# Block-sparse attention followed by a SwiGLU block: dense masked scores replaced by per-block lists of key blocks

## The chip, the cores and the metric

One Trainium2 chip, and of it one core. The time of a kernel is the device time of one execution in microseconds (us). Lower is better. A profile shows one execution, from its first to its last instruction (the span).

## What is computed

Attention over 4 batches of 8 heads, 768 positions, 64 values per head, then RMS normalisation and a SwiGLU feed-forward block. Positions are grouped in 24 blocks of 32. A query block may attend to its neighbours at a distance of at most one block, to the first and the last block, and to three sampled blocks that arrive as data. The first and the last query block attend to everything.

```python
B, H, S, D = q.shape                      # 4, 8, 768, 64
scores = scale * np.matmul(q, k.transpose(0, 1, 3, 2))
mask = np.abs(blk_i - blk_j) <= 1
mask = mask | (blk_i == 0) | (blk_j == 0) | (blk_i == n_blocks - 1) | (blk_j == n_blocks - 1)
for qb in range(n_blocks):
    for kb in sampled_blocks[qb]:         # three per query block, known at run time alone
        mask[qb * 32:(qb + 1) * 32, kb * 32:(kb + 1) * 32] = True
attn = softmax(np.where(mask, scores, -1e9));  x = attn @ v        # heads side by side: 3072 x 512
xn = x / rms(x) * rms_g
out = (silu(xn @ w_gate) * (xn @ w_val)) @ w_out                   # 512 -> 1536 -> 512
```

## The kernel before

The work is cut into 24 tiles of 128 queries (six a batch) and these into ten units: batch 0 has three units of one tile and one of three, every other batch two of three. A unit goes through attention, normalisation and the feed-forward block.

Scores are dense. The mask is folded into the product: each head's 64 rows of K and of Q are widened by 24 rows (one per block), so that one matmul over 88 rows gives the score plus 0 for an allowed pair of blocks, and a large negative number for the rest. `aug` holds the widened rows as they come from memory (`fill`, `fillk`, `fillq`), `X` the same turned: in batch 0 by TensorE transposes (`tpx` L258, copied out by `evx`), later by a DMA transpose issued on SP (`turn` L245). Positions are dealt to partitions so that one load piece is 1536 contiguous bytes. For a unit of `nt` tiles, `qk` (L276), `exp` (L296) and `av` (L310) do, for each pair of heads and each of the six key tiles:

```python
nc.tensor.matmul(out=s_[:, e, j * w:(j + 1) * w],                  # qk: w = nt * 128 columns
                 lhsT=x[0:KQ, 0, e, jt * P:(jt + 1) * P],
                 rhs=x[0:KQ, 1, e, c0 * P:c0 * P + w], start=True, stop=True)
nc.scalar.activation(out=pts[u, pr][...], in_=s_[...], func=AF.Exp, scale=SCALE)
nc.tensor.matmul(out=o_[:, t, e, :], lhsT=pt[:, jt, e, t * P:(t + 1) * P],   # av: 65 columns
                 rhs=va[:, (2 * pr + e) * NC + jt, 0:D + 1], ...)  # column 65 of V is 1: the row sum
```

V stays in SBUF (`vaug`, filled by `pad_v`). `xo` (L321, L322) divides by the row sum, `sq`, `rsq` (on POOL, L343) and `xq` (L350) normalise, `tr` (L361) and `cp`, or from unit 4 on a DMA transpose `xt` (L376), turn the tile. The feed-forward block is `proj` (L388, gate and value, 12 column groups for a unit of three tiles), `th` (L397, ACT), `uu` (L403, DVE), `hp` (L414, DVE), `yy` (L427) and `yo` (L437, ACT or DVE), with the store on SP. The weights are loaded and cast to 16 bits by DMAs that POOL issues: `load_w` (L211, four quarters of gate and value) and `load_wo` (L215, two halves).

The order of all of it is written down when the program is built. Each piece is an `op` with a cost for each engine that may do it, things it waits for, buffers and PSUM banks that it takes and frees, and a priority. A planner loop deals them out by their earliest start; what it deals is recorded at once, so each engine's queue is a fixed order, and an engine waits wherever the chip is later than the plan. `idle` (L128) puts matmuls without use into the TensorE queue where the plan expects TensorE to wait early on. `gate_sync` holds the loads of batch 1 on the SP queue until parts of the weights have landed.

Of the kernel before, what the change touches and what calls it, by code (L numbers as in the profile page):

```python
# [17 lines left out]
def kernel(  # L18
# [11 lines left out]
):  # L30
    nc = tc.nc
    SIMOUT = None
# [3 lines left out]
    NC = S // P  # L36
    DM = H * D
# [3 lines left out]
    MASKV = -32768.0  # L41
    SCALE = 1.0 / (D ** 0.5)
    NRND = sampled_blocks.shape[1]
    KQ = D + NB
    NSLOT, NAUG, NRAW, NOPEN = 5, 2, 3, 2
    AHEAD, HURRY, HURU = 0.8, ("av", "xo", "sq", "rsq", "xq", "tr", "cp"), 0
    NSTARV, ZPAT, NG2 = 3, 32.0, 4
    AH = {"uu": 0.3, "hp": 0.3}
    WARM = (11, 10, 2)
    HD = NC * D // 2  # L50
    UNITS = [(0, 0, 1), (0, 1, 1), (0, 2, 1), (0, 3, 3)]
    UNITS += [(b, c, 3) for b in range(1, B) for c in (0, 3)]
    NU = len(UNITS)
    HG = [(b, c // 3) for b, c, n in UNITS]
# [5 lines left out]
    psum = ctx.enter_context(tc.tile_pool(name="psum", bufs=1, space=bass.MemoryType.PSUM))  # L60
    PS = psum.tile([P, 8, 512], FP32, name="PS")

    def bank16(n):
        return PS[:, n].bitcast(BF16)

    qv = q.rearrange("b h (p c) d -> b p h (c d)", c=NC)
    kv = k.rearrange("b h (p c) d -> b p h (c d)", c=NC)
    vv = v.rearrange("b h (p c) d -> b p h (c d)", c=NC)

    raws = {}  # L70
    aug = [const.tile([P, 2, 2, NC, P], BF16, name=f"aug{i}") for i in range(NAUG)]
    XA = const.tile([P, NSLOT, 2, 2, S], BF16, name="XA")
    X = [XA[:, i] for i in range(NSLOT)]
    vaug = [const.tile([P, H * NC, D + 2], BF16, name=f"vaug{i}") for i in range(2)]

    def load(g, i):
        b, pr = divmod(g, NP)
        if i == 0:
            raws[g] = raw.tile([P, 3, 2, NC * D], FP32, name="qkv", tag="qkv")
        nc.sync.dma_start(out=raws[g][:, i], in_=(kv, qv, vv)[i][b, :, 2 * pr:2 * pr + 2, :])  # L80

    TI = work.tile([P, DM], I32, name="ti", tag="yo", bufs=3)
    TF = work.tile([P, DM], FP32, name="tf", tag="yo", bufs=3)
    TB = work.tile([P, 2 * DM], BF16, name="tb", tag="yo", bufs=3)
    samp_i = TI[0:32, 200:200 + 2 * NRND]
# [3 lines left out]
    nc.scalar.dma_start(out=samp_i[0:NB, :], in_=s64)  # L89
    A = [raw.tile([P, 3, 2, NC * D], FP32, name="qkv", tag="qkv") for g in range(3)]  # L90
    def load0(g, i, e=slice(0, 2), x=None, eng=nc.sync):
        x = x or slice(0, HD if i == 1 else NC * D)
        eng.dma_start(
            out=A[g][:, i, e, x], in_=(kv, qv, vv)[i][0, :, 2 * g:2 * g + 2][:, e, x])

    load0(0, 0, slice(0, 1))
    load0(0, 0, slice(1, 2))
    load0(0, 1, x=slice(0, D), eng=nc.scalar)
    load0(0, 1, x=slice(D, HD))
    load0(1, 0)  # L100
    load0(1, 1)
    gB = const.tile([P, DM], FP32, name="gB")
    scr = const.tile([P, 16], BF16, name="scr")
    scf = const.tile([P, 1], FP32, name="scf")
# [9 lines left out]
    zt = const.tile([P, 512], BF16, name="zt")  # L114
    nc.vector.memset(zt[:, 0:P], 0.0)  # L115
    kmask = const.tile([P, NC, NB], BF16, name="kmask")
    nc.vector.memset(kmask, 1.0)
    ident = const.tile([P, P], BF16, name="ident")
    nc.vector.memset(ident, 0.0)
    Bm = TB[0:32, 0:32]  # L120
    nc.vector.memset(Bm, 1.0)
# [4 lines left out]
    def idle(n, bk=7):  # L126
        for i in range(n):
            nc.tensor.matmul(out=PS[:, bk, 0:P], lhsT=zt[:, 0:P], rhs=zt[:, 0:P], start=True, stop=True)  # L128

    idle(WARM[0])  # L130
    ji = TI[0:32, 0:NRND * 32].rearrange("p (r j) -> p r j", r=NRND)
    nc.gpsimd.iota(ji, pattern=[[0, NRND], [1, 32]], base=0, channel_multiplier=0)
    nc.gpsimd.affine_select(
        out=kmask, in_=kmask, compare_op=ALU.is_ge, fill=0.0,
        base=0, pattern=[[1, NC], [-32, NB]], channel_multiplier=NC)
# [664 lines left out]
```

## Time and profile before

| what | value |
|---|---|
| three runs | 309.01, 309.51 and 314.6 us; median 309.51 us |
| the profiled execution, first to last instruction | 307.2 us (its own total is not listed; the median of the runs lies 2.3 us above its span) |
| busy: TensorE matmul (PE), weight load (PEld) | 299.6 us (98%), 200.2 us |
| busy: ACT, DVE, POOL | 203.7, 192.3, 24.4 us |
| scores, L276 | 480 matmuls, 81.1 us busy |
| exponentials, L296 | 192 instructions (188 in pt, 4 in ph), 145.8 us |
| probabilities times V, L310 | 1152 matmuls |
| gate and value, L388; output, L427 | 960 and 300 matmuls |
| DMA | 42.42 MB in 70,661 packets |

PE is TensorE's matmul row, PEld its weight load, DVE VectorE, ACT ScalarE, POOL GpSimd, SP the queue that issues most DMAs; L276 is line 276 of the kernel. A matmul's duration is its latency and overlaps the next one's, so what one costs is read from runs of equal matmuls in the chain of waits (36 of L310 in 1.15 us), not from its mean.

### The profile page before, as it was taken

To read this page: it belongs to the slowest core of one execution; us is meant where nothing else is said; L and a number is where in the kernel's file an instruction comes from. 1 tells how busy PE (TensorE), PEld (TensorE's weight loads), DVE (VectorE), ACT (ScalarE), POOL (GpSimd) and SP (SyncE) were. 2 spreads that over 40 slices of the span, in tenths; PEclk is the share of its full clock that TensorE was granted. 3 is DMA by queue.
4 is the path that set the end of the run, shared out by engine and by line. 5 is a ranking of instruction groups with operands and counts; after the bars stand their busy time and mean duration, and the time that the engine had idled before them with its cause. 6 is when DMAs were issued, how large, how long until landed. Compare 5 with 4: busy or idle time off the path is not lost.

```text
span 307.2 us, 7350 instructions
## 1 busy us (share of the span) xinstructions
PE 299.6 (98%) x3033; PEld 200.2 (65%) x3062; DVE 192.3 (63%) x435; ACT 203.7 (66%) x319; POOL 24.4 (8%) x43
## 2 busy tenths in 40 slices
PE   8999999999999999999999999999999999999994
PEld 7998888766666566666666666666666546556543
DVE  6687766857779678756754753674389607727500
ACT  5999875678977878787877787878833143233221
POOL 3566000100001001001000100010000000000000
PEclk9999999999999999999999999999999999999999
DMA  7999999999999999940894030003010050010022
GB/s 207 370 231 172 215 268 228 228 333 247 262 285 271 227 205 222 242 155 3 173 157 101 0 87 2 34 3 85 2 36 1 20 158 12 0 70 0 0 105 104
DMA packets 70661, 42.42 MB, mean 138 GB/s; under 512 B 48356, under 2 KB 67556, under 8 KB 70628
## 3 DMA queue, kind: packets, MB, share of 16 engines
q1 hardware_dynamic: 64528, 37.17, 49.2%
q0 software_dynamic: 5792, 4.72, 10.0%
q8 instruction: 24, 0.39, 0.6%
q10 hardware_dynamic: 308, 0.07, 0.1%
q14 instruction: 9, 0.07, 0.1%
HBM read 28.57 MB, written 6.29 MB: 114 GB/s over the span
## 4 chain that ended last, share of the span: by engine, by line
PE 96%; ACT 2%; issue 1%; DVE 0%; ACTq 0%
PE PS L388 40%; PE PS L276 20%; PE PS L427 20%; PE PS L310 12%; PE PS L258 2%; ACT pt L296 1%; PE PS L128 1%; PE PS L361 0%; ACT th L397 0%; PE PS L153 0%; ACT yo L437 0%; PE PS L183 0%; DVE zt L115 0%; ACTq L437 0%
## 5 line engine op out<-in xcount | busy, mean ns | idle before, releaser
L296 ACT ACTIVATE pt<-PS 128x768 bf16<-128x768 f32 x188 | 142.8, 812 | 32.2 <-PE PS L276 31.5
L403 DVE SCALAR_TENSOR_TENSOR uu<-th,PS 128x384 bf16<-128x384 bf16 x96 | 53.0, 554 | 58.7 <-ACT th L397 55.7
L276 PE MATMUL PS<-XA 88*128 88x384 bf16 (+1 forms) x480 | 81.1, 293 | 0.7 <-ACT pt L296 0.6
L388 PE MATMUL PS<-xn,wv 128*128 128x384 bf16 (+1 forms) x480 | 75.5, 293 | 0.0
L388 PE MATMUL PS<-xn,wg 128*128 128x384 bf16 (+1 forms) x480 | 75.1, 294 | 0.0
L397 ACT ACTIVATE th<-PS 128x384 bf16<-128x384 f32 x96 | 47.2, 493 | 34.8 <-PE PS L388 32.1
L427 PE MATMUL PS<-wo,hp 128*128 128x512 bf16 (+1 forms) x271 | 65.4, 370 | 1.5
L414 DVE TENSOR_TENSOR hp<-uu,PS 128x384 bf16<-128x384 bf16 x96 | 51.4, 551 | 14.2 <-PE PS L388 14.0
L388 PEld LDWEIGHTS <-wv 128*128 128x128 bf16 x480 | 41.6, 97 | 23.3
L388 PEld LDWEIGHTS <-wg 128*128 128x128 bf16 x480 | 41.4, 98 | 22.5
L276 PEld LDWEIGHTS <-XA 88*128 88x128 bf16 x480 | 39.2, 97 | 21.4 <-issue 1.8
L427 PEld LDWEIGHTS <-hp 128*128 128x128 bf16 x300 | 29.1, 98 | 27.0
L310 PEld LDWEIGHTS <-pt 128*128 128x128 bf16 x1128 | 40.5, 97 | 5.8
L310 PE MATMUL PS<-vaug,pt 128*128 128x65 bf16 x1128 | 42.1, 193 | 0.0
L437 ACT ACTIVATE yo<-PS 128x512 f32<-128x512 f32 (+1 forms) x22 | 12.7, 578 | 27.9 <-PE PS L427 27.2
L343 POOL TENSOR_TENSOR rs<-ms,nhalf 128x3 f32<-128x3 f32 (+1 forms) x10 | 7.9, 785 | 203.8 <-DVE ms L335 203.8
L322 DVE TENSOR_TENSOR xo<-PS,rz 128x384 f32<-128x384 f32 (+1 forms) x40 | 19.1, 478 | 1.4
L350 DVE SCALAR_TENSOR_TENSOR xq<-xo,rs,gB 128x512 bf16<-128x512 f32 x24 | 17.3, 747 | 2.3 <-POOL rs L343 2.3
L335 DVE CUSTOM_DVE_ANT_0 sc<-xo 128x512 bf16<-128x512 f32 (+1 forms) x24 | 16.1, 669 | 0.2
L321 DVE RECIPROCAL rz<-PS 128x6 f32<-128x6 f32 (+1 forms) x40 | 7.4, 186 | 12.8 <-PE PS L310 12.6
L112 DVE CAST aug<-qkv 128x768 bf16<-128x768 f32 (+1 forms) x28 | 14.5, 538 | 0.1
L112 DVE COPY XA<-PS 88x768 bf16<-88x768 bf16 (+2 forms) x17 | 8.4, 516 | 2.3 <-PE PS L258 2.2
(60 smaller groups left out, 74.5 us busy)
## 6 DMA issues: line engine op xcount, KB each, us to landing
out_dram<-yo SPq DMA_DIRECT2D x23, 256.0 KB, 2.4
qkv<-in_v_dram SPq DMA_DIRECT2D x15, 384.0 KB, 6.1
qkv<-in_k_dram SPq DMA_DIRECT2D x14, 384.0 KB, 5.6
qkv<-in_q_dram SPq DMA_DIRECT2D x12, 384.0 KB, 5.7
wg<-in_moe_w_gate_dram POOLq DMA_DIRECT2D x4, 384.0 KB, 7.3
wv<-in_moe_w_val_dram POOLq DMA_DIRECT2D x4, 384.0 KB, 8.4
wo<-in_moe_w_out_dram POOLq DMA_DIRECT2D x2, 768.0 KB, 19.0
q<-in_q_dram SPq DMA_DIRECT2D x1, 768.0 KB
```

The lines of the kernel that those rows point to most:

```text
L112: nc.vector.tensor_copy(out=out, in_=in_)
L276: nc.tensor.matmul(out=s_[:, e, j * w:(j + 1) * w], lhsT=x[0:KQ, 0, e, jt * P:(jt + 1) * P], rhs=x[0:KQ, 1, e, c0 * P:c0 * P + w], start=T ...
L296: nc.scalar.activation(out=pts[u, pr][:, g * kt:(g + 1) * kt].rearrange("p j e w -> p e j w"), in_=s_[:, :, 0:kt * w].rearrange("p e (j w) ...
L310: nc.tensor.matmul(out=o_[:, t, e, :], lhsT=pt[:, jt, e, t * P:(t + 1) * P], rhs=va[:, (2 * pr + e) * NC + jt, 0:D + 1], start=(jt == 0), ...
L322: nc.vector.tensor_tensor(out=xos[u][:, :, 2 * pr:2 * pr + 2, :], in0=o_[:, :, :, 0:D], in1=rz.unsqueeze(3).to_broadcast([P, nt, 2, D]), o ...
L335: nc.vector.tensor_tensor_reduce(out=sc[:, z], in0=x, in1=x, scale=1.0 / DM, scalar=mss[u][:, 0:1] if nt == 1 and t else 1e-6, op0=ALU.mul ...
L350: nc.vector.scalar_tensor_tensor(out=xqs[u][:, t, :], in0=xos[u][:, t].rearrange("p h d -> p (h d)"), scalar=mss[u][:, t:t + 1], in1=gB, o ...
L388: nc.tensor.matmul(out=p_[:, j, :].rearrange("p (t w) -> p t w", w=P), lhsT=w_[:, c, f_ * P:(f_ + 1) * P], rhs=xns[u][:, :, c, :], start=( ...
L397: nc.scalar.activation(out=t_, in_=tiles["gp", u, f], func=AF.Tanh, scale=0.5)
L403: nc.vector.scalar_tensor_tensor(out=t_, in0=tiles.pop(("th", u, f)), scalar=1.0, in1=tiles.pop(("gp", u, f)), op0=ALU.add, op1=ALU.mult)
L414: nc.vector.tensor_tensor(out=hps[u][:, f * fg:(f + 1) * fg, :], in0=tiles.pop(("uu", u, f)), in1=tiles.pop(("vp", u, f)), op=ALU.mult)
L427: nc.tensor.matmul(out=tiles["yp", u, t, h], lhsT=hps[u][:, f, t * P:(t + 1) * P], rhs=wo[:, f, x], start=(f == 0), stop=(f == NF - 1))
```

## The change

Attention is rewritten; the feed-forward block, its lines (L388 becomes L538, L427 becomes L577) and the units of work stay. The order of tiles inside a batch becomes 5, 0, 1, 2, 3, 4, and tile 5, written `AT`, now holds query blocks 0, 23, 21 and 22; tile n holds blocks 4n+1 to 4n+4.

- A tile's keys. For each of the four query blocks x of a tile, `kg` slot x is a list of 128 keys: three sampled blocks and one fixed block. Two more slots (4 and 5), each shared by two query blocks, hold two neighbour blocks and the first and last block. `kg_fixed` copies the fixed parts (four copies for each half tile, on DVE or ACT). `kg_sampled` copies the sampled ones, one instruction a block, at an address read from a table in a register (half on POOL, half on ACT, each preceded by one register instruction).
- A tile's values. `store_v` writes V with its column of ones as rows of 1040 bytes to DRAM (`vrows`). `gather_v` fetches for one query block the 128 rows of its list by an indirect DMA on POOL, with row numbers `idx` that the start of the kernel computes on DVE; entries that repeat point to rows of zeros. `pair_v` loads the shared slots by plain DMAs on SP.
- Scores. `q_diag` lays the queries of two heads block-diagonally (`qbd`), so that one matmul over 128 rows gives both heads: four matmuls of 64 columns and two of 128 for a pair of heads of an ordinary tile. `AT` has six matmuls of 128 columns over all keys for blocks 0 and 23, and two of 64 and one of 128 for its other blocks (`qka`).
- `exp` then has two instructions of 512 values for four heads (`expa` has four of 512, 256, 64 and 128 values for two heads); `av` has 24 matmuls for four heads of an ordinary tile and 36 for `AT`, each of 65 columns as before.
- K is turned for two heads at a time without padding; K, V and Q are loaded in pieces of 512, 512 and 256 bytes. The first weight load now stands behind the store of V of batch 0 in the plan, the second, third and fourth quarter behind gathers (`WAFTER`).
- Fixed buffers: three `ptb`, one `pab`, three `qbd`, two `kg`, three `vg`. The first three kinds are set to zero on POOL at the start.

The core of the diff (the planner loop is the same but for its constants):

```diff
-    def qk(u, pr, g, bk):
-        b, c0, nt = UNITS[u]
-        x, kt, w = X[(b * NP + pr) % NSLOT], KT[nt], nt * P
...
-                nc.tensor.matmul(
-                    out=s_[:, e, j * w:(j + 1) * w],
-                    lhsT=x[0:KQ, 0, e, jt * P:(jt + 1) * P],
-                    rhs=x[0:KQ, 1, e, c0 * P:c0 * P + w], start=True, stop=True)
+    def kg_sampled(b, n, xs, eng):
...
+        for x, r in xs:
+            kb = koff[(blocks(n)[x] - 1) * NR + r]
+            copy(eng, kg[:, x, :, :, r, :], kt[:, :, :, bass.ds(kb, 16)])
+    def store_v(b):
+        (nc.sync if b else nc.scalar).dma_start(
+            out=vrows[b][0:S, :].rearrange("(t p c) f -> p t (c f)", p=P, c=2),
+            in_=vaug.rearrange("p t c h d -> p t (c h d)"))
+    def gather_v(b, n, x):
+        c_ = blocks(n)[x] - 1
+        nc.gpsimd.indirect_dma_start(
+            out=new_vg(b, n)[:, x, :], out_offset=None, in_=vrows[b][:, :],
+            in_offset=bass.IndirectOffsetOnAxis(ap=idx[:, c_:c_ + 1], axis=0))
+    def pair_v(b, n):
...
+            nc.sync.dma_start(out=vg[0:64, 5 - g, :], in_=vrows[b][lo:lo + 64, :])
...
+    def qk(b, n, pp, bk):
...
+        for pl in range(2):
+            pr = 2 * pp + pl
+            o_ = s_[:, 2 * pl:2 * pl + 2]
+            for i in range(4):
+                qmm(o_[:, :, i * 32:(i + 1) * 32], kg[:, i, pr], qb, i, 1, pr)
+            for g in range(2):
+                lo = P + (1 - g) * 64
+                qmm(o_[:, :, lo:lo + 64], kg[:, 5 - g, pr], qb, 2 * g, 2, pr)
...
+        for a in range(4):
...
+                vs = [vg[:, x, h * (D + 1):(h + 1) * (D + 1)] for x in range(6)]
+            for x, v_ in enumerate(vs):
+                nc.tensor.matmul(
+                    out=o_[:, a, :], lhsT=p_[:, a, x * P:(x + 1) * P], rhs=v_,
+                    start=(x == 0), stop=(x == len(vs) - 1))
...
+    for t in QBD:
+        nc.gpsimd.memset(t, 0.0)
...
+    for t in PTB + PAB:
+        nc.gpsimd.memset(t, 0.0)
...
-    kv = k.rearrange("b h (p c) d -> b p h (c d)", c=NC)
+    kvv = [t.rearrange("b h (t p c) d -> b p (h t) (c d)", p=P, c=2) for t in (k, v)]
+    qvv = q.rearrange("b h (n p) d -> b n p h d", p=P)
```

## The prediction, written before the run

> **What bounds the kernel now.** I read the page's busy times first, then its chain of waits.
>
> ```profile
> PE 299.6 (98%) x3033; PEld 200.2 (65%) x3062; DVE 192.3 (63%) x435; ACT 203.7 (66%) x319; POOL 24.4 (8%) x43
> PE 96%; ACT 2%; issue 1%; DVE 0%; ACTq 0%
> PE PS L388 40%; PE PS L276 20%; PE PS L427 20%; PE PS L310 12%; PE PS L258 2%; ACT pt L296 1%; PE PS L128 1%; PE PS L361 0%; ACT th L397 0%; PE PS L153 0%; ACT yo L437 0%; PE PS L183 0%; DVE zt L115 0%; ACTq L437 0%
> ```
>
> TensorE is the chain for 96% of the span, so a matmul that goes is time saved, as long as nothing else makes TensorE wait. The longest pieces of the chain in order of time, and the chain of the last 84 us alone, give the price of one matmul in a row of equal ones.
>
> ```profile
> 24.85 0.67 PE PS L388 x12
> 31.70 1.15 PE PS L310 x36
> 73.25 0.65 PE PS L276 x4
> 75.85 1.30 PE PS L388 x8
> ...
> 223.98 0.79 PE PS L310 x25
> 224.77 16.25 PE PS L388 x100
> 241.02 0.05 issue
> 241.07 10.31 PE PS L427 x47
> ```
>
> So 384 columns cost 0.1625 us, 128 columns 0.0558, 65 columns 0.0319, 512 columns about 0.2165. The last attention matmul ends at 224.77; what follows is feed-forward work alone, 78.6 us of it to 303.4, and 3.8 us of last copy and store.
>
> Then the engines and the DMA by stretches of time, the POOL instructions by shape, and the DMA queues:
>
> ```profile
> 16.00:34.00 18.00, 17.44 (x338) 15.98 (x336) 14.72 (x50) 16.50 (x26) 10.83 (x16) 1.00 1.24 194
> 80.00:130.00 50.00, 49.54 (x522) 32.23 (x527) 37.83 (x82) 40.04 (x61) 1.89 (x2) 1.00 1.11 245
> ```
>
> ```profile
> L343 POOL TENSOR_TENSOR rs<-ms,nhalf 128x3 f32<-128x3 f32 x7 | 6.1, 878 | 199.7 <-DVE ms L335 199.7
> L211 POOL DMA_DIRECT2D wg<-in_moe_w_gate_dram x4 | 3.3, 818 | 0.0
> L215 POOL DMA_DIRECT2D wo<-in_moe_w_out_dram x2 | 1.7, 845 | 0.0
> L110 POOL CAST aug<-wo 128x768 bf16<-128x768 f32 x1 | 0.8, 827 | 0.6 <-PE PS L258 0.6
> L110 POOL CAST aug<-qkv 128x384 bf16<-128x384 f32 x2 | 1.0, 507 | 2.7 <-PE PS L258 1.4 <-DMA qkv<-in_q_dram 1.3
> ```
>
> ```profile
> q1 hardware_dynamic: 64528, 37.17, 49.2%
> q0 software_dynamic: 5792, 4.72, 10.0%
> ```
>
> After length, the stretches list PE, PEld, DVE, ACT and POOL busy, then TensorE's granted clock, the DMA share and GB/s. ACT and DVE are four fifths busy; POOL is nearly free after 34 us; the DMA share passes 1.1. Per packet, on all 16 engines, q1 takes 0.492 x 307.2 / 64,528 = 2.34 ns and q0 30.7 us / 5792 = 5.3 ns.
>
> **The change on TensorE.** Scores go from 336 x 0.1625 + 144 x 0.0558 = 62.6 us to 352 matmuls of 64 columns and 272 of 128: 352 x 0.0319 + 272 x 0.0558 = 26.4. V: 1152 to 1248, +3.1. Transposes of K and Q: 96 to 48 at 0.056, from 5.8 (2% of the chain) to 2.7. Masks by matmul (L153, L183): -0.9. That is 38 us less useful work. But the new queue holds 340 matmuls without use (19.0 us) for 38 before: they stand where the plan itself expects TensorE to wait.
>
> I added these prices along the new queue, in its order. The first V matmul stands at 24.1 us, the first feed-forward one at 30.0 (24.85 on the clock before), the first score of batch 1 at 84.2, its last V matmul at 105.3, the last of all at 198.1, and 78.7 of feed-forward follow. That tail is the 78.6 measured before. So the comparison is short: when does the last V matmul end, against 224.8? It is 198.1 plus the waits, and 26.7 us of waits eat the gain.
>
> **The start.** K, two pieces of Q and V are 3.67 MB; at the 240 GB/s of the first 10 us K lands at 8.5 and V at 17. POOL must first clear 16,896 elements. No row shows a long clear on POOL: its casts rise 0.32 us over 384 elements, 0.83 ns each, so 14 us above and half of it, 6.9, below. A clear reads nothing and writes 2 bytes, so I take 6.9. With 6 us of small work and table loading ahead (the same table reached DVE at 2.8 before) POOL is free at 13; its half of K, the turn and the copy out end at 15.5. Then come the copies of `AT` and of the next tile, a piece of V (18.5) and three weight issues among more copies: the first weight goes at 21.7 (13.9 before), the first gathers at 25 to 27. They queue behind three weight pieces, 3 x 512 x 5.3 ns = 8 us, and land at 32, for 24.1 in the queue: 8 us of wait.
>
> **Batch 1.** Its V, K and Q loads and the store of V stand on SP behind waits for weights and the first output store. Packets of q0 from 21.7 to the last weight: 5632 weight packets and 18 gathers of 128, 29.9 + 12.2 = 42.1, plus 2.4 to land: 66. Then output of the first unit and V's store, so V is in DRAM at 73. Behind the gathers that wait for it stand on POOL the key copies of the next tiles and `rsq`, which the feed-forward block waits for; behind `pair_v` on SP wait the loads of K and Q.
>
> The order of POOL has, from there, 22 gathers and 16.9 us of other work in batch 1, then 44 and 38.4: 33 key copies a batch at 0.25 and a register step, which no row shows (0 to 0.1, taken as 0.06), `q_diag`, two instructions for `rsq`. A gather: nothing shows one. The weight issues take 0.75 to 0.85 for 512 or 768 rows; below, a quarter of that many rows can't be dearer: 0.75; above, reading the row numbers may cost as much again as the dearest issue, 1.69. I take 1.0, nearer to the issue rows, which do the same but for the numbers. So the last gather of batch 1 goes at 73 + 38.9 = 112, and its V matmuls end at 116 (2.4 landing, 1.5 of matmuls); TensorE alone would be at 105.3 + 8 = 113.
>
> The Trainium skill ("SBUF — State Buffer", section "SBUF: two separate sides") speaks against such gathers: POOL can't write descriptors while DVE runs a two-port copy, and a transfer of 620 ns was seen to take 3100. Here eight weight issues took 0.74 to 0.95 us while DVE was busy for 14.72 of 18 us; were each gather 3.1 us instead, the sum below would come to an estimated 421.
>
> **The rest.** From 105.3 to 198.1 TensorE has 92.8 us. POOL has 82.4, ACT 67 (0.06 us + 0.83 ns an element, from exponentials back to back; 112 smaller ones and 178 + 46 key copies for the 192 old), DVE 65. So the key copies cost nothing there, hidden by TensorE's 92.8; were the feed-forward work not there as cover, POOL's 82.4 would set the pace. Four engines at 70 to 100% under a fixed order trip over each other: before, 180 to 224 lost 0.3 us with three at 51 to 99%. I take 4, with 0 to 12.
>
> **The sum.** 116 + 92.8 + 4 = 212.8, that is 12 us before 224.8; span 295.2, and with the 2.3 us by which the median of the runs lies above the profiled span, **297.5**.
>
> **The rivals.** (1) *POOL becomes the bound; slower.* The last V matmul by POOL is at 73 + 16.9 + 38.4 + 3.9 + 66 g = 132.2 + 66 g. TensorE's 212.8 is reached at g = 1.22, the old 224.8 at 1.40, 2% slower at about 1.49; at the upper bound 1.69 it is 243.7, and the time 328.4. For: 88 gathers on an engine that was idle. Against: the issue rows stay under 0.95 under load. 0.18.
>
> (2) *The DMA queues become the bound.* Smaller pieces of K, V and Q, and V three times over: a batch has 20,672 packets on q1 and 2816 on q0, 48.4 + 14.9 = 63.3 us, 190 for three, from the first load of batch 1 at about 52. At the share of 1.24 that is 153 us, until 205: hidden. At 1.11 it is 171, until 223, last V matmul 227: 311.7; if gathers also land late, 320. For: the share is over 1.1 already. Against: 256- and 512-byte packets should cost less than q1's mean. 0.18.
>
> (3) *The start costs more.* Clears at 0.83 ns make everything 7 us later, 304.5; the change does what it says and most of it is given back in the first 73 us. 0.12.
>
> **How the numbers follow.** The forecast has 0.52. Its own range is 286 (first wait 3 instead of 8, gathers at 0.75, V stored 5 us earlier: last V matmul at 201, 24 us earlier than before) to 305 (the 12 for 4). Into the range for 8 in 10 I take rivals 2 and 3 and rival 1 up to g = 1.6 (237.8, so 322.5): 285 to 323. About 2% is what a measurement of this kernel tells from no change: faster under 303.3, slower over 315.7. Faster: forecast and a little of rival 3, 0.54. Same: most of 3 and half of 2, 0.21. Slower: rival 1 and the rest of 2, 0.25.
>
> **What would show it.** Right: the tail after the last V matmul is 78 to 79 us; that matmul ends near 213; a gather is about 1.0 us in POOL's rows; TensorE's waits lie before 116, and name POOL or a DMA. The first step is wrong if 64-column matmuls cost over 0.04 us; the start, if POOL's clears take 14 us or the first V matmul isn't near 32; the batch 1 step, if its first gather isn't near 73. If POOL is over 90% busy from 80 us on, rival 1 holds; if gathers and loads land after over 8 us while POOL idles, rival 2.

## The result, and the profile after

The changed kernel takes 400.5 us (398.1 to 401.9, four runs) where the kernel before, run beside it, takes 309.6: a ratio of 1.294, 95% interval 1.289 to 1.299. The prediction was 297.5, between 285 and 323. On another chip, in the last set of experiments, it took 393.2 us (392.9 to 393.3) against 308.7, a ratio of 1.273 (1.271 to 1.275). Why it depends on the chip is told with that set; up to there a run of the first set is set against 400.5 and one of the second and third against 393.2.

The page of the changed kernel, profiled execution with a span of 398.8 us: busy times, DMA queues, and the chain that ended last by engine and by line.

```profile
PE 317.4 (80%) x3544; PEld 221.4 (56%) x3544; DVE 217.1 (54%) x519; ACT 191.4 (48%) x524; POOL 191.3 (48%) x309
...
q1 hardware_dynamic: 88344, 39.44, 41.1%
q0 software_dynamic: 10016, 16.44, 19.7%
...
PE 34%; POOL 10%; DVE 7%; issue 6%; DMA 4%; ACT 3%; SPq 1%; another core or an unknown queue 1%; POOLq 0%; ACTq 0%; DVEq 0%
PE PS L538 19%; PE PS L577 9%; POOL vg L356 4%; PE PS L460 4%; DMA raw<-in_k_dram 3%; POOL kg L125 3%; DVE kg L127 2%; POOL qbd L125 1%; PE PS L392 1%; DVE uu L553 1%; DVE xq L503 1%; SPq L311 1%; ACT kg L123 1%; DVE xo L471 1%; PE PS L390
```

TensorE is busy for 80% of the span, where it was 98%. The chain can be followed back to 130.0 us only, so its shares add up to two thirds of the span; TensorE has 34% of the span, about half of what was followed, where it had 96%. The rest of the chain goes round all engines and is no single bound: POOL 10%, DVE 7%, issue 6%, DMA 4%. No engine but TensorE is busy for more than 54%. The queue q1 has 37% more packets than before, q0 73% more.

The chain of the last part, in order of time:

```profile
315.93 0.73 PE PS L460 x24
316.65 16.90 PE PS L538 x104
...
381.59 10.37 PE PS L577 x48
392.66 2.81 DMA out_dram<-yo
```

The last V matmul, L460, ends at 316.65 and TensorE's feed-forward work alone follows, until 392 on the chain. So the tail has kept its length and the whole loss lies ahead of it: 316.6 against 224.8.

The same two stretches of time as were shown of before, and one inside batch 1. After the length come PE, PEld, DVE, ACT and POOL busy, then the granted clock, DMA share and GB/s:

```profile
16.00:34.00 18.00, 12.46 (x153) 12.13 (x154) 9.67 (x17) 6.88 (x21) 15.42 (x19) 0.71 0.50 110
80.00:130.00 50.00, 41.80 (x474) 29.37 (x472) 27.63 (x63) 24.81 (x51) 20.81 (x29) 0.92 0.91 215
160.00:180.00 20.00, 12.12 (x193) 10.87 (x194) 12.47 (x30) 12.68 (x42) 16.70 (x31) 0.58 0.85 198
```

In the first stretch TensorE is busy for 12.5 us of 18 (17.4 before) while POOL has its longest work, in the second for 41.8 of 50 (49.5 before). The granted clock, 1.00 before in the first two, is now 0.71 and 0.92, and 0.58 in the third.

POOL's instructions by shape (count, busy time and mean ns of one, idle time before them):

```profile
L356 POOL DMA_INDIRECT vg<-vrows,idx x88 | 90.3, 1027 | 34.1 <-issue 19.2 <-PE PS L392 5.2 <-PE PS L460 3.5
L125 POOL COPY kg<-KT 128x128 bf16 x132 | 38.4, 357 | 23.9 <-PE PS L392 15.1 <-PE PS L390 7.0 <-DVE QT L127 1.5
...
L227 POOL MEMSET ptb<- 128x3072 bf16 x3 | 8.8, 2975 | 0.0
...
L227 POOL MEMSET pab<- 128x4608 bf16 x1 | 4.2, 4217 | 0.0
```

A gather takes 1.03 us, and of the 34.1 us of idle time ahead of them 19.2 are a fixed 0.30 us behind the one before ("issue"): back to back they come every 1.25 us. The clears of `ptb` and `pab` take 13.0 us, with 2.8 for the three `qbd` 15.8.

**Where the waits lie.** I took the start of every V matmul from the trace and subtracted the place that the same matmul has in TensorE's queue by the prediction's own prices. The difference is what waits and slower matmuls have added so far:

| stretch | measured, us | price in the queue, us | added, us |
|---|---|---|---|
| start to first V matmul | 46.2 | 24.1 | 22.1 |
| batch 0, first to last V matmul | 51.3 | 30.1 | 21.2 |
| batch 0 to batch 1 | 46.4 | 33.4 | 13.0 |
| batch 1 | 43.6 | 17.7 | 25.9 |
| batch 1 to 2, batch 2 | 59.8 | 42.5 | 17.3 |
| batch 2 to 3, batch 3 | 69.2 | 50.3 | 18.9 |
| all, to the last V matmul | 316.5 | 198.1 | 118.4 |

The queue's 198.1 us are 26.7 below the old 224.8. So 118.4 - 26.7 = 91.7 us is the loss, as measured (400.5 - 309.6 = 90.9). The prediction allowed 8 us at the start and 14.7 in all. About 78 of the 118.4 us are idle time of TensorE (398.8 - 317.4 = 81.4 in the span, less 3.6 behind its last matmul); the other 40 are matmuls that took longer than their price.

Two chains on the queues of SP and POOL show how a batch comes late. First SP's queue (start, length, operation) around the loads of batch 1, then POOL's instructions in the same stretch, then two of SP's waits over the whole run (us in total, times, longest):

```profile
60.26 9.75 SPq L364 DMA_DIRECT2D vg<-vrows  x4
70.11 0.73 SPq L251 DMA_DIRECT2D scr<-wv  x1
70.95 4.01 SPq L100 DMA_DIRECT2D raw<-in_v_dram  x2
...
94.95 1.43 SPq L595 DMA_DIRECT2D out_dram<-yo  x3
...
97.11 0.77 SPq L316 DMA_DIRECT2D vrows<-vaug  x1
...
104.63 3.81 SPq L306 DMA_TRANSPOSE KT<-krow  x1
...
117.40 6.22 SPq L112 DMA_DIRECT2D raw<-in_q_dram  x5
...
129.27 5.00 SPq L311 DMA_TRANSPOSE QT<-qrow  x1
```

```profile
106.11 1.10 POOL L356 DMA_INDIRECT vg<-vrows,idx  x1 [1.51 <-DMA vrows<-vaug]
...
136.30 1.78 POOL L125 COPY qbd<-QT 64x256 bf16<-64x256 bf16 x4 [15.63 <-DMA QT<-qrow]
```

```profile
SPq L595 <- DVE yo L589: 34.1, 6, 15.3
SPq L364 <- PE PS L460: 32.7, 6, 13.2
```

V of batch 1 is loaded at 70.95. What held SP before it is `pair_v` of batch 0 (L364), whose buffers a V matmul sets free at 68.9; the wait for a piece of the weights behind it (L251) starts at 70.11 and holds nothing more. V's second half has landed at 87.4, its last cast stands on ACT at 95.29, the store goes at 97.11, and POOL's first gather of batch 1 starts at 106.11, having waited for it. SP itself stood from 79.7 to 94.95 for an output tile, the 15.3 us of the list. Q of batch 1 is loaded from 117.40, behind `pair_v`, turned at 129.27, and POOL has waited 15.63 us for it at 136.30. TensorE fills this gap with feed-forward work; what is added there is 13.0 us. More is added inside batches 0 and 1, where the chain runs from one tile to the next. TensorE's waits (us in total, times, longest):

```profile
PE PS L538 <- DVE uu L553: 17.4, 11, 5.9
...
PE PS L460 <- DVE xo L471: 7.6, 7, 1.8
PE PS L538 <- DVE hp L564: 5.8, 2, 5.1
```

A score matmul, an exponential on ACT, a V matmul and DVE's `xo` follow each other through few banks and buffers, and in a fixed order a late one makes the next late. That is how I read these waits; no run changes the banks, the buffers or TensorE's order alone.

### The profile page after: what moved, and what is told of

Same layout as the page of the kernel before. It is cut to its first block, busy times and chain, and to the rows that moved or that the text cites. A ratio compares the mean times of both kernels' runs of the same rounds, so it can differ in the third digit from the quotient of the medians.

```text
span 398.8 us, 9391 instructions
## 1 busy us (share of the span) xinstructions
PE 317.4 (80%) x3544; PEld 221.4 (56%) x3544; DVE 217.1 (54%) x519; ACT 191.4 (48%) x524; POOL 191.3 (48%) x309
## 2 busy tenths in 40 slices
DMA packets 99141, 57.48 MB, mean 144 GB/s; under 512 B 56600, under 2 KB 91672, under 8 KB 99096
## 4 chain that ended last, share of the span: by engine, by line
PE 34%; POOL 10%; DVE 7%; issue 6%; DMA 4%; ACT 3%; SPq 1%; another core or an unknown queue 1%; POOLq 0%; ACTq 0%; DVEq 0%
PE PS L538 19%; PE PS L577 9%; POOL vg L356 4%; PE PS L460 4%; DMA raw<-in_k_dram 3%; POOL kg L125 3%; DVE kg L127 2%; POOL qbd L125 1%; PE PS L392 1%; DVE uu L553 1%; DVE xq L503 1%; SPq L311 1%; ACT kg L123 1%; DVE xo L471 1%; PE PS L390 1%
## 5 line engine op out<-in xcount | busy, mean ns | idle before, releaser
L356 POOL DMA_INDIRECT vg<-vrows,idx x88 | 90.3, 1027 | 34.1 <-issue 19.2
L538 PE MATMUL PS<-xn,wg 128*128 128x384 bf16 (+1 forms) x480 | 79.7, 308 | 23.1 <-DVE uu L553 17.4
L547 ACT ACTIVATE th<-PS 128x384 bf16<-128x384 f32 x96 | 46.7, 489 | 92.1 <-PE PS L538 77.9
L538 PE MATMUL PS<-xn,wv 128*128 128x384 bf16 (+1 forms) x480 | 78.8, 303 | 6.5 <-DVE hp L564 5.8
L577 PE MATMUL PS<-wo,hp 128*128 128x512 bf16 (+1 forms) x300 | 70.3, 372 | 2.4 <-ACT yo L587 0.7
L538 PEld LDWEIGHTS <-wg 128*128 128x128 bf16 x480 | 42.7, 102 | 49.9 <-issue 30.5
L123 ACT COPY kg<-KT 128x128 bf16 (+2 forms) x224 | 54.5, 362 | 19.0 <-PE PS L392 9.6
L538 PEld LDWEIGHTS <-wv 128*128 128x128 bf16 x480 | 42.1, 101 | 31.5 <-issue 10.8
L460 PE MATMUL PS<-vg,ptb 128*128 128x65 bf16 x960 | 43.6, 207 | 12.5 <-DVE xo L471 7.3
L460 PEld LDWEIGHTS <-ptb 128*128 128x128 bf16 x960 | 40.8, 107 | 16.9 <-issue 14.5
L125 POOL COPY kg<-KT 128x128 bf16 x132 | 38.4, 357 | 23.9 <-PE PS L392 15.1
L418 ACT ACTIVATE ptb<-PS 128x512 bf16<-128x512 f32 x80 | 43.1, 598 | 9.2 <-PE PS L392 4.8
L577 PEld LDWEIGHTS <-hp 128*128 128x128 bf16 x300 | 28.7, 98 | 30.1 <-issue 4.1
L390 PE MATMUL PS<-qbd,kg 128*128 128x64 bf16 x352 | 27.8, 205 | 8.6 <-ACT pab L445 3.0
L390 PEld LDWEIGHTS <-kg 128*128 128x128 bf16 x352 | 22.8, 107 | 16.0 <-issue 8.8
L125 POOL COPY qbd<-QT 64x256 bf16<-64x256 bf16 (+1 forms) x32 | 17.6, 563 | 26.3 <-DMA QT<-qrow 24.6
L144 PE MATMUL PS<-zt 128*128 128x128 bf16 x340 | 25.3, 244 | 2.7 <-DVE QT L127 1.5
L392 PE MATMUL PS<-qbd,kg 128*128 128x128 bf16 x176 | 26.3, 238 | 0.4 <-issue 0.4
```

Of the source, the lines that this page charges most:

```text
L123: nc.scalar.copy(out=out, in_=in_)
L125: nc.gpsimd.tensor_copy(out=out, in_=in_)
L356: nc.gpsimd.indirect_dma_start(out=new_vg(b, n)[:, x, :], out_offset=None, in_=vrows[b][:, :], in_offset=bass.IndirectOffsetOnAxis(ap=idx[ ...
L390: nc.tensor.matmul(out=out_, lhsT=kg, rhs=rhs[:, 0], start=True, stop=True)
L392: nc.tensor.matmul(out=out_.rearrange("p h (i x) -> p i h x", i=m), lhsT=kg, rhs=rhs, start=True, stop=True)
L418: nc.scalar.activation(out=o_, in_=i_, func=AF.Exp, scale=SCALE)
```

## Experiments

Each kernel has the changed kernel's order on every engine, except where the planner's costs are changed (e6, e9 and its repeat e17), where transfers move to another queue (e7, e9, e10, e13, e17) or where the kernel before is edited (e15, e18); line numbers shift by a few. "First V" and "last V" are TensorE's first and last V matmul.

**First set: one suspect at a time.**

*e1, no gathers.* In `gather_v`, with `seen` an empty set at the start:

```diff
+        if (held["vg", (b, n)][1], x) in seen:
+            return
+        seen.add((held["vg", (b, n)][1], x))
         nc.gpsimd.indirect_dma_start(
```

> Leaves out 76 of the 88 gathers of V rows (the first into each place of each buffer stays, so the V rows used later are old ones); every other instruction and its order stay. Theory G (the gathers on POOL set the pace, 76 x 1.25 us = 95 us of POOL's time): the last V matmul falls from 316.5 by 60 us or more and the time to 340 or less. Theory O (the fixed order was written with cheaper prices, so that each batch has its own last input, and POOL's gathers are one of several): the first V matmul moves by about 3 to 6 us (two or three gathers less ahead of it), the batches inside shrink by 20 to 40 us together, and the gap from batch 0 to batch 1 (46 us) stays within 8 us of what it was, because the loads of batch 1 wait on SP: time 355 to 380.

Measured: 366.6 us, 34 less; last V at 282.5. Theory G falls. The gap from batch 0 to batch 1 is 43.2 us, as theory O had it, but the first V matmul, at 48.8, is 2.6 us later and not 3 to 6 earlier; what is added after the first V matmul falls from 96.3 to 59.6 us. So the gathers are the largest single cost, but more than half of the loss is not theirs.

*e2, no key copies.* In `kg_sampled`, with `done` an empty set at the start:

```diff
+            if (held["kg", (b, n)][1], x, r) in done:
+                continue
+            done.add((held["kg", (b, n)][1], x, r))
             kb = koff[(blocks(n)[x] - 1) * NR + r]
```

> Leaves out 240 of the 264 copies of sampled key blocks at register addresses (the first into each place of each buffer stays), on POOL and ACT; everything else in the same order. Theory K (the key copies pace the attention, 120 x 0.34 us on each of POOL and ACT): the excess inside the batches, 72 us over TensorE's own prices, falls by 40 us or more, time 355 or less. Theory O: 10 to 30 us off, time 370 to 390, and the gaps between the batches stay.

Measured: 398.5 us, 2 less. Both theories missed: some 80 us of copies on POOL and ACT are taken away and nothing comes of it. Theory K falls.

*e3, early clears.*

```diff
     nc.vector.tensor_copy(out=itf[:, 4:54], in_=it[:, 4:54])
+    PTB = [const.tile([P, 4, NT * P], BF16, name=f"ptb{i}") for i in range(NPT)]
...
+    for t in PTB:
+        nc.vector.memset(t, 0.0)
+    for t in QBD + PAB:
+        nc.gpsimd.memset(t, 0.0)
...
-    for t in QBD:
-        nc.gpsimd.memset(t, 0.0)
...
-    for t in PTB + PAB:
-        nc.gpsimd.memset(t, 0.0)
```

> The same clears, set ahead of the register loads: three score buffers on DVE and the rest on POOL, in the time in which both wait for the table. Theory S (the start's delay is carried through to the end): first V matmul from 46 to 32 to 36, and the last one and the time fall by the same 10 to 14 us: 386 to 390. Theory O with other inputs late: the first V matmul comes earlier by 10 or more, but the end falls by less than 6 us, because batch 1's inputs wait on something else than the start.

Measured: 395.4 us, 5 less, and the first V did not move (46.7). POOL is through with its clears at 8.1 instead of 24.6, but ACT's first work starts at 16.25 (13.77 before), since its register loads now follow a later table on DVE; the first gather goes at 37.3 instead of 40.7. Theory S in its first form missed; so did the other, which had the first V matmul 10 us earlier.

*e4, one batch's data.*

```diff
     def load_kv(b, i, hf):
+        if b:
+            return
...
     def turn_k(b):
+        KTs[b] = KTs[0]
+        return
...
     def store_v(b):
+        if b:
+            vrows[b] = vrows[0]
+            return
```

`load_q`, `fill_k`, `fill_v` and `fill_q` are left out for b > 0 as `load_kv` is, and `turn_q` as `turn_k`; the waits for weights ahead of the loads go with them.

> Batches 1 to 3 use the K, Q and V rows of batch 0: their loads, casts, turns and stores of V are left out, the gathers, key copies, matmuls and all orders stay. Theory B (the loads and turns that stand in SP's order behind stores, weights and buffers set the start of each batch): the gap from batch 0 to batch 1 falls from 46 us to its price in the queue, about 33, the three gaps together by 20 to 25 us, and with the casts gone the batches by some more: time 360 to 378. Theory G: the gathers still pace, so less than 10 us is gained, time over 390.

Measured: 393.8 us, 7 less. The gap from batch 0 to 1 fell only from 46.4 to 43.0 us. Theory B's 20 to 25 us are not there while the gathers are; theory G's range, over 390, holds here.

**Second set: together, and mended.** Second and third set ran on a chip that is like that of the last set in what tells the chips apart, so that 393.2 us is taken for the changed kernel.

*e5, the four edits together.*

> The four edits of the first experiments together: 76 gathers and 240 key copies left out, clears early, batches 1 to 3 on the rows of batch 0; TensorE's queue is the same. Theory A (the four add up, each hiding the others): alone they gave 34, 2, 5 and 7 us; with each other's cover gone they give 60 to 90 together, time 310 to 340, and TensorE idles less than 25 us. Theory O (what is left is in the order and in the chains of score, exponential, V matmul and copy on ACT and DVE): not more than the plain sum of 48, time 350 or more, and TensorE's waits name ACT and DVE.

Measured: 332.5 us. Alone the four gave 34, 2, 5 and 7 us, together 61 to 68: each was hidden by the others, as theory A says, whose 310 to 340 holds; only TensorE's idle time, 38 us (330.4 - 292.1), is over the 25 that it allowed. The busy times of its page and TensorE's longest waits:

```profile
PE 292.1 (88%) x3524; PEld 206.8 (63%) x3544; DVE 202.7 (61%) x509; ACT 159.4 (48%) x394; POOL 63.9 (19%) x103
```

```profile
PE PS L563 <- DVE uu L578: 7.4, 13, 1.2
PE PS L301 <- DVE krow L131: 4.0, 1, 4.0
PE PS L301 <- ACT krow L127: 3.4, 1, 3.4
```

POOL is at 19% and TensorE at 88%, and 24 us of the loss are still there.

*e6, replanned.* Early clears, and the planner's costs: for `kf` 1.22 on DVE and 1.2 on ACT (0.6 and 0.9 before), for `qd` 1.3 on POOL and 0.9 on DVE (for `AT` 2.4 and 1.6), and

```diff
-                op(("gv",) + T + (x,), {"POOL": 1.0}, [("st", b)], (1.1, order, x),
+                op(("gv",) + T + (x,), {"POOL": 1.25}, [("st", b)], (1.1, order, x),
...
-    free = {"PE": 3.5, "ACT": 4.0, "DVE": 5.5, "POOL": 9.0, "DMA": 2.1, "SP": 6.0}
+    free = {"PE": 3.5, "ACT": 17.0, "DVE": 14.0, "POOL": 12.0, "DMA": 2.1, "SP": 6.0}
```

> Nothing left out: early clears, and the planner is given the measured costs (gather 1.25 us, fixed key copies 1.2, block-diagonal copies 1.3 to 2.4, first free times 17 on ACT, 14 on DVE, 12 on POOL), so that it writes another order. Theory O1 (wrong costs made the order bad; a right one hides the work): TensorE's idle time of 81 us falls by half, time 345 to 365. Theory O2 (no order hides it: the inputs of a batch come too late and the buffers hold too few tiles): less than 15 us below the run with early clears alone, 380 to 396.

Measured: 380.3 us, 13 under 393.2. First V at 33.2 and first feed-forward matmul at 50.4 (45.8 and 60.8 in the changed kernel on its chip), but the additions inside batches 0 and 1 stay: 19.5 and 21.9 us by the prices of its own queue, 18.5 and 20.9 in the changed kernel on its chip. Wrong costs are a small part; theory O2 holds, at the lower edge of its range.

*e7, stores on ACT.*

```diff
-            nc.sync.dma_start(out=out[r0:r0 + 32 * m, x], in_=o[32 * i:32 * (i + m), :])
+            nc.scalar.dma_start(out=out[r0:r0 + 32 * m, x], in_=o[32 * i:32 * (i + m), :])
```

> The output stores are issued by ACT instead of SP, all else and all orders as they were. Theory B (loads, the store of V and the turns of batch 1 stand on SP behind output stores, 79.6 to 95.0 us): the second half of K and the store of V go about 15 us earlier, the first gather of batch 1 from 106 to about 92, the first V matmul of batch 1 from 144 to 130 to 135, time 385 to 393. If the gathers and the turn of Q are held by buffers instead, the gap stays and the time is within 4 us of 400.

Measured: 393.9 us. Against 400.5 that looked like a gain, against the 393.2 of the changed kernel on a like chip it is none. V of batch 1 is stored at 93.91 here and at 94.02 there: it waits for ACT's last cast, not for the stores ahead of it on SP. I had read SP's queue wrongly: the stores stood in front, but the input behind them was late for a cause of its own. The first gather of batch 1 did come earlier, at 99.3 for 103.1, and the batch's first V matmul at 137.1 for 140.5; the end did not follow. So this input alone does not set the end.

*e8, start.* Early clears, and the register loads at their first use:

```diff
+    def offset(k_):
+        if k_ not in koff:
+            e, lo = k_ % 2, k_ // 2 // 3 * 3
+            eng = (nc.gpsimd, nc.scalar)[e]
...
+        return koff[k_]
...
-            kb = koff[(blocks(n)[x] - 1) * NR + r]
+            kb = offset((blocks(n)[x] - 1) * NR + r)
```

> Early clears, and each register load stands in front of the first key copies that use it instead of all at the start; orders as they were. Theory S (the start is set by clears and register loads on POOL and ACT): K is turned by 18 instead of 26, the first V matmul at 36 to 40 instead of 46, and the end falls by 8 to 12 us, 388 to 392. If the first V matmul stays at 44 to 47, it waits for the gathers' landing behind the weight pieces, not for POOL or ACT.

Measured: 387.3 us, 6 under 393.2; first V at 39.2, inside the range of theory S, last V at 302.9. So 6.6 us earlier at the first V are 6.2 at the last, under the 8 to 12 that theory S expected. Clears alone had not moved the first V (e3); no run moved the register loads alone.

**Third set.**

*e9, combined:* e6's planner with first free times of 10, 14 and 9, e7 and e8, and the loads of batch 1 gated on weight pieces 1 and 2 instead of 3 and 4.

> Nothing left out: early clears, register loads at their first use, output stores on ACT, the planner with measured costs, and the loads of batch 1 held only until the second and third quarter of the weights. If the causes are separate, the gains over 400 add: 20 (new order, which has the 5 of the clears in it), 8 (register loads), 7 (stores), some for the loads: 358 to 366. If the input chain of batch 1 (V in DRAM, gathers, Q turned) decides, the later parts give less than half of that: 370 to 378. No theory has it under 335, since each tile still needs four gathers of 1.25 us.

Measured: 372.5 us, and 376.7 in the last set (e17), both in the second theory's 370 to 378. But the 358 to 366 for separate causes were reckoned from 400. From 393.2 the single gains are 13 (e6), at most 6 (e8) and nothing (e7), which leaves 374 or a little more, about what was measured. So e9 doesn't tell the two theories apart. It is the best version that leaves nothing out, and by e17 22% slower than before.

*e10, rows by SP.*

```diff
-        nc.gpsimd.indirect_dma_start(
-            out=new_vg(b, n)[:, x, :], out_offset=None, in_=vrows[b][:, :],
-            in_offset=bass.IndirectOffsetOnAxis(ap=idx[:, c_:c_ + 1], axis=0))
+        lo = 32 * min(c_, NB - 4)
+        nc.sync.dma_start(out=new_vg(b, n)[:, x, :], in_=vrows[b][lo:lo + P, :])
```

> With the stores on ACT (393.9 us), each gather is replaced by a plain transfer of 128 rows in one piece, issued by SP; the bytes are the same, the rows are not those of the lists. Theory G1 (POOL's 1.25 us an instruction is what a gather costs): POOL is free of 110 us and the time falls by 20 to 35 to 360 to 374, as it did without gathers. Theory G2 (what costs is the traffic and the landing of 11.7 MB): less than 8 us off, 386 or more. It could also rise if SP becomes the queue that holds things up (88 more issues of about 0.5 us).

Measured: 374.0 us, 20 under e7 with the same bytes moved (57.47 against 57.48 MB). Most of what e1 gained is gained here too, so the bytes are not what a gather costs. What it costs goes with its issue on POOL; but the edit also moves the rows to another queue and takes them from one piece, and it doesn't part these from POOL's time.

*e11, neither gathers nor key copies* (e1 and e2).

> Leaves out both the 76 gathers and the 240 sampled key copies, all else as in the changed kernel. Alone they gave 34 and 2 us. If the key copies cost nothing because gathers come last, they show up now: 345 to 357. If they are hidden by other work in any case: 362 to 366.

Measured: 363.1 us, 3.5 under e1. As the second theory had it, the key copies are hidden even when the gathers are gone.

*e12, five edits* (e5 and e8's register loads).

> The four edits together (332.5 us) and the register loads at first use. Theory S: the start still carries 18 us over TensorE's own prices there, and falls by 6 to 10: time 322 to 327. If the first V matmul stays near 42, the start waits for transfers: 330 or more.

Measured: 331.8 us, though the first V came from 41.8 to 38.1. Theory S missed its 322 to 327: batch 0's last V is at 80.3 instead of 81.9 and the end where it was.

**Fourth set: what is left, and what a gather costs elsewhere.**

*e13, no gather on POOL:* e12 with its remaining twelve gathers as in e10.

> The kernel with the four edits and deferred register loads (331.8 us), its last twelve gathers, those of the first three tiles, replaced by plain transfers of 128 rows issued by SP. Theory S (POOL's gathers among the weight issues hold the start, 14 + 12 us over TensorE's prices): first V matmul from 38 to 30 to 35, first feed-forward matmul from 53 to 38 to 45, time 316 to 325. Theory O (the order itself, with 33 us of feed-forward work between batches 0 and 1 and a tail of 78 us): the start comes earlier, the end stays at 328 to 333.

Measured: 335.2 us, first V at 38.7, first feed-forward matmul at 57.5. Theory S falls for what is left, and theory O, which had an earlier start and 328 to 333, is missed too. SP issues V rows from 32.5 on, while POOL issues seven weight pieces from 28.3 to 34.8, and TensorE waits for V rows until 49.5, 7.0 us in all, 3.9 at the longest. Ahead of the first V matmul stand 84 matmuls without use, 4.7 us, which the planner put where it expected a wait.

*e14, no gathers and one batch's data* (e1 and e4).

> The changed kernel without 76 gathers and with batches 1 to 3 on the rows of batch 0; clears, register loads and key copies stay. Without gathers it was 366.6, with all four edits 332.5. If loads, casts and turns hold it once the gathers are gone (theory B): 335 to 345. If clears and key copies hold it: 355 or more.

Measured: 348.5 us, 18 under e1, where e4 alone gave 7; between the two ranges, so that the next 16 us, down to e5, belong to clears and key copies.

*e15, the kernel before with 88 gathers that nobody reads.*

```diff
     def rsq(u):
...
+        for j in range(11 if u > 1 else 0):
+            nc.gpsimd.indirect_dma_start(
+                out=gt[:, j % 3, :], out_offset=None,
+                in_=k.rearrange("b h (s x) d -> (b h s) (x d)", x=4),
+                in_offset=bass.IndirectOffsetOnAxis(ap=gi, axis=0))
```

> The kernel before with 88 gathers of 128 rows of 1 KB, 11 behind each of the last 8 rs instructions on POOL, into a tile that nobody reads: POOL is idle there for 20 to 36 us each time. Theory P (a gather costs only where an instruction in a fixed order waits behind it): POOL is busy 90 us more and the time stays within 1%, 306 to 313. Theory R (the gathers slow others as well, by traffic or by a shared port): 2% or more, over 316.

Measured: 345.6 to 352.6 us in four runs, median 351.1 (the two quickest have a mean of 347.6), against 309.1. Theory P falls clearly: gathers on an idle engine, whose rows nobody reads, cost the old kernel 38 to 42 us. Near one of its stalls, DVE's, ACT's and POOL's instructions (start, length, what ended the idle time before):

```profile
203.58 0.56 DVE L411 SCALAR_TENSOR_TENSOR uu<-th,PS 128x384 bf16<-128x384 bf16 x1 [1.26 <-ACT pt L299]
212.57 0.20 DVE L324 RECIPROCAL rz<-PS 128x6 f32<-128x6 f32 x1 [8.44 <-remote]
```

```profile
203.44 0.81 ACT L299 ACTIVATE pt<-PS 128x768 bf16<-128x768 f32 x1
212.62 1.51 ACT L299 ACTIVATE pt<-PS 128x768 bf16<-128x768 f32 x2 [8.37 <-remote]
```

```profile
204.78 0.95 POOL L349 DMA_INDIRECT gt<-in_k_dram,gi  x1 [0.30 <-issue]
...
210.59 0.95 POOL L349 DMA_INDIRECT gt<-in_k_dram,gi  x1 [0.30 <-issue]
```

DVE's `rz` needs V matmuls that end at 204.9, and ACT's `pt` scores that end at 207.1. Both start at 212.6, together, 8.4 us after their last work, and what they waited for is put down to "remote". The trace's semaphore events explain it: five updates that TensorE made with matmuls from 204.7 to 208.7 all arrived between 212.55 and 212.75, 1 us after the last gather of the row had ended on POOL. I then counted TensorE's semaphore updates that are missing from the trace or come later than 0.1 us after their instruction. Before: none of 463. Changed kernel, first profile: 93 of 472, all while a gather ran or within 2 us behind one. e2, e3 and e4, 87 to 104; here 80 of 463. e6 to e9: 6 to 13. e13, without any gather but on the chip of e15: none of 406. Sets with many and sets with few ran on different chips, and that is what the last set was for.

**Fifth set: three kernels again, on one chip.**

*e16, the changed kernel as it is.*

> The changed kernel itself, beside the two that follow. If late semaphore updates belong to the kernel (its stores on SP, its order): they are as many as in its first profile, about 97 of 472 on TensorE, and the time is 398 to 402. If they belong to the execution or its chip: on a chip without them fewer than 15, and the time is 5 to 12 us shorter, 388 to 396.

*e17, the combined version e9.*

> The version with nothing left out and all mendings (372.5 in its first run). If the late updates go with the chip, it has them here when the changed kernel has them, and is then slower than 375; its distance to the changed kernel on this chip is 16 to 24 us where there are none. If they go with the kernel it has none, and 370 to 375.

*e18, the kernel before with gathers, as e15.*

> The kernel before with the 88 unread gathers (351.1 against 309.1). If late updates go with the chip and cost the 42 us: on a chip without them 309 to 325. If the gathers cost by the DMA queues, in which the old kernel's turns of K, Q and activations stand: 340 or more on any chip.

Measured: the changed kernel 393.2 us with 7 late updates of 471; the combined version 376.7 (374.7 to 380.3) with 9 of 487, ratio to before 1.224 (1.217 to 1.230); the old kernel with gathers 325.2 (322.8 to 327.6) with 1 of 463, ratio 1.050 (1.045 to 1.056). So the many late updates go with the execution and its chip and not with the kernel; only kernels with gathers have them. They go with 7 of the changed kernel's 91 us and with 22 to 26 of the 38 to 42 that gathers cost the old one. Why some chips have them was not found out, nor whether the recording of the profile has a part in it.

The other 16.5 us of the old kernel with gathers, 325.2 against 308.7, are mostly plain in the profile. SP's queue at the same two turns, first in the kernel before, then in e18, and e18's waits on TensorE:

```profile
67.60 8.97 SPq L245 DMA_TRANSPOSE XA<-aug  x2
```

```profile
67.83 15.22 SPq L248 DMA_TRANSPOSE XA<-aug  x2
```

```profile
PE PS L396 <- DMA xn<-xq: 8.4, 1, 8.4
PE PS L279 <- DMA XA<-aug: 5.7, 1, 5.7
```

Two turns of K and Q took 15.22 us where they took 8.97, all eighteen turns 90.7 us on SP where they took 65.6, and TensorE waited 8.4 and 5.7 us for turned tiles. It is the prediction's second rival, in a kernel where nothing else was changed, if smaller than the 340 us expected of it. In the changed kernel the turns show little of it: its six turns of K and Q took 24.8 us, and 23.7 without gathers (e1).

**What is settled.** On one scale, each step an experiment that takes away more: 393 for the changed kernel, 367 without gathers, 349 without loads and turns of later batches, 332 without clears and key copies, 309 for the kernel before. (The second and third ran on chips with late updates, but with twelve gathers left they had few.) What makes the last 23 us is open: neither POOL's gathers nor the register loads (e12, e13); what e12 still has is 26 us of additions up to the end of batch 0 and the order itself, and no run changed TensorE's order alone.

## Why the prediction was wrong

**Right.** TensorE's prices: 24 V matmuls at the full clock take 0.73 us, 0.030 each (0.0319 in the sum). The tail was to be 78 to 79 us: from the last V matmul at 316.5 to TensorE's last at 394.9 it is 78.4. The comparison built on it holds too: 26.7 us of waits eat the gain, the rest is loss. The savings that it lists add up to 37 us and not 38 (62.6 - 26.4 - 3.1 + 3.1 + 0.9); nothing rests on it, since 198.1 was added up along the queue.

**The start: too low.** The clears were taken at 6.9 us, half of what the casts' slope gave, because a clear reads nothing; they took 15.8, 0.94 ns an element, above my upper bound of 14. The Trainium skill ("VectorE: DVE Perf Modes", section "Zero memsets can be issued as uint32 (trn2)") says for VectorE that a memset takes one cycle per element whatever its type. POOL's rows, 2975 ns for 3072 two-byte elements and 4217 for 4608, are 0.97 and 0.92 ns an element, more than the 0.83 of the casts and no less for two bytes; no run clears another type on POOL. Read so, the rule spoke against the halving. The register loads were not priced at all: ACT, with 33 of them, starts its first work at 13.77. First V matmul 46.2 instead of 32. Rival 3 was this and nearly right in size for the clears (7 us more, measured 8.9), but its time, 304.5, took the rest to be as forecast. Moving clears and register loads gave back 6.6 of the 14 us (e8); what holds the other 7 is open (e12, e13).

**Batch 1: the step that failed most.** The first term of the sum, the end of its V matmuls at 116, measured 187.5 (46.2 + 51.3 + 46.4 + 43.6 in the table): 71.5 of the 103.7 us by which the last V matmul of all came late (316.5 for 212.8). The sum had waits of 8 us at the start and of 3 for the gathers of batch 1, and none inside batches 0 and 1, where 21.2 and 25.9 us were added. It also had V in DRAM at 73; the first gather waited until 106.1. I counted packets behind the first weight issue, at the speed of the queue. The path was longer: the weight issues stand among POOL's gathers, from 34.7 to 77.1, V's load stands behind `pair_v`, which waits for V matmuls of batch 0, then V waits for casts on POOL and ACT behind other work, then for its store. And K's and Q's loads, casts and turns, of which the prediction only said what they wait behind, had no time in the sum: Q is turned at 134. How much of the 71.5 us this path makes is not shown: in e7 the first gather came 3.8 us earlier without an earlier end, and the gap to batch 1 is only 13.0 of what was added.

**Gathers.** 1.0 us was the instruction (1.03 measured); the 0.30 us behind each was missed, so the pitch was 1.25, just over the 1.22 from which rival 1 decides. But rival 1 as a bound on POOL's time was not what happened: POOL is 48% busy, and 54% from 80 to 320 us. Plain transfers on SP in their place gave 20 us (e10), leaving the gathers out 27 to 34 (e1). None of the 88 took more than 1.56 us; that the estimate of 421, from 3.1 us for each, lies nearer to 400.5 than the forecast is luck. (Two of the eight weight issues that the prediction set against it, the 0.95 among them, go before 16 us, ahead of the stretch of which it gave DVE's busy time.) Key copies were taken at 0.25 us and a register step of 0.06 that no run shows by itself; together they measured 0.36 on POOL and 0.33 on ACT, and without most of them the time fell by 2 (e2).

**The rest.** 4 us were allowed from 105.3 on, 12 at most, since the old kernel, with three engines at 51 to 99%, had lost 0.3 us there. That row came from a kernel whose loads were mostly done by then (DMA share 0.17 from 180 to 224). Here batches 2 and 3 add 36 us after batch 1.

**The clock.** The prediction took the old granted clock of 1.00 for granted. Here its mean is 0.901: it falls in stretches in which TensorE waits, and then the matmuls cost more. Two groups of 24 V matmuls of batch 1:

```profile
145.87 0.89 PE L460 MATMUL PS<-vg,ptb 128*128 128x65 bf16 x24
...
161.46 1.48 PE L460 MATMUL PS<-vg,ptb 128*128 128x65 bf16 x24 [0.73 <-DVE rz L470]
```

0.89 and 1.48 us for the same work. Over the stretches of 20 us, busy time times what the clock lacks to 1.00 adds up to some 28 us, an estimate, of the 40 by which matmuls took longer than their price. The Trainium skill ("TensorE: Matmul & The Clock Gate", section "HAM oscillation — how this bites in real kernels") describes this loop, with waits longer than a window of 3.4 us that halve the clock. The trace agrees on the loop but not on the length: from 144 to 178 no wait of TensorE is over 1.82 us, and the clock is 0.58 from 160 to 180, with TensorE busy for 12.1 of 20 us. The busy share alone doesn't tell either: from 140 to 160 it is busy for 12.9 of 20 us at a clock of 0.99. e5, with few waits, has 0.974 in the mean. No run changed the clock alone, so how much of the loss is the clock's own isn't shown.

**How the cases were put together.** Three rivals had a chance each, as if one of them at most would come. Parts of all three came at once, with the forecast's gain as well: a gather's 1.25 us on POOL, loads that land late (V of batch 1 more than 12 us after its issue; gathers in the median after 4.2, in e16), and the start. They hid each other: four edits that gave 48 us one by one gave 61 to 68 together. With chances for single causes the range ended at 323.

## What to carry to other kernels

Where many in-order queues carry one fixed order, time an input's whole path, load, cast, store or turn, gather, copy, through every queue that it stands in, and add up the rivals before giving any a chance of its own. A TensorE at 98% that becomes one at 80% can pay twice, by waits and by its clock: 1.00 and 0.901 here. Removing one suspect at a time understated them here, 48 us for 61 to 68; remove them together as well, and run the unchanged kernel beside each set.

## What the hardware showed that I had not expected

An indirect gather of 128 rows takes POOL 0.94 us at the least, 1.03 in the mean, and 0.30 more before the next one starts. Gathers that nobody reads cost a kernel bound by TensorE 5% on one chip and 12 to 14% on another. On some chips TensorE's semaphore updates came in bursts, up to 8 us late, while gathers ran, and DVE and ACT stood still together; on another the same two programs had 7 and 1 such updates where they had had 93 and 80. A copy from a register address costs no more than a fixed one: on ACT both kinds of key copy of 128 elements take 333 ns.
